# A windowed attention and feed-forward kernel: scores over 64 rows, values by three query blocks, loads by feature halves, and a planner that counts instructions

## Chip, cores and metric

The kernel runs on one core of a Trainium2 chip. The metric is the time of the program on the device in microseconds, the median of several runs; lower is better. A core has a matrix engine (TensorE, PE in the profile), a vector engine (VectorE, DVE), a scalar engine (ScalarE, ACT), GpSimd (POOL) and a sequencer that issues DMAs (SyncE, SP). Every engine works through its own instruction queue in order.

## What is computed

Attention over 8 batches, 8 heads, 576 positions and 64 features, in which a query sees the keys within 32 positions of it and 8 global positions, and the queries of the global positions see every key. Its result, 4608 tokens of 512 features, goes through a feed-forward layer of width 2048 with softplus.

```python
scores = scale * np.matmul(q, k.transpose(0, 1, 3, 2))
mask = np.abs(pos[:, None] - pos[None, :]) <= window
mask = mask | is_global[:, None] | is_global[None, :]
scores = np.where(mask, scores, -1000000000.0)
attn = np.exp(scores - np.max(scores, axis=-1, keepdims=True))
attn = attn / (np.sum(attn, axis=-1, keepdims=True) + 1e-09)
attn_out = np.matmul(attn, v)
x = attn_out.transpose(0, 2, 1, 3).reshape(B * S, H * D)
h = x @ w_in
g = np.maximum(h, 0.0) + np.log1p(np.exp(-np.abs(h)))
return g @ w_out
```

## The kernel before

**Tiles.** A batch's 576 positions are 18 blocks of 32; the 8 batches make 144 blocks. Four blocks in a row are a *pair* (its 8 heads lie as two halves, so the tile has two planes), four pairs are a *stage* of 512 tokens, and there are nine stages. The stages' values and feed-forward products are numbered m = 0 to 8.

**Loads.** For each batch, `load_qk` (line 241) brings q and k into `stage0` and `stage1`, two heads to a group of 32 partitions: four DMAs for each tensor, 2,304 contiguous pieces of 512 bytes. `load_v` (246) brings v in eight DMAs of 256-byte pieces. All are issued from SP's queue, apart from half of the first batch's q and k, which go out from ScalarE's. The output stores (813) stand in SP's queue too. GpSimd issues the weights' loads (843, 847). A batch's q and k can be loaded only after the batch before has been cast out of the same buffer.

**Preparing a batch.** q, k and v are cast to bf16 (line 414, the copy helper, on ScalarE, GpSimd or VectorE). `turn` (474, 484, 486) transposes q and k in 32 by 32 blocks on VectorE. `pick` (495) gathers the global positions' rows of q and k with 144 small products (each with a weight load); `tg` and `fill` put the picked keys into the slots between the blocks of `kx`. A query block thus finds its own block, its two neighbours and the global keys in four neighbouring slots of 32.

**Scores.** `sc` (622) computes a pair's scores: for each block, 2 halves of the features by 8 heads, products of 32 rows by 32 columns over 128 columns, two of which add up to one head's scores. The first four pairs add the mask with a third product (the identity with the mask); the others add it on VectorE (629). Then on VectorE the maximum (639), on GpSimd the difference (647), on ScalarE the exponential (660), on VectorE the sum and its reciprocal (667, 669), on GpSimd the product with the reciprocal (676, `pn`), and on VectorE a transpose (686, `pt`).

**Global queries.** `sg` (548) computes their scores against all keys, in three products (two feature halves, then the row mask), `mx` and `gexp` (556, 565) the maximum and the exponential with its sum (read from ScalarE's accumulator), `tpg` (577) the transpose, `ov` (585) the product with v, per head half and block, and `gv` (590) the division.

**Values.** `val` (770) forms a stage's attention output in four PSUM banks: for each two query blocks one product with the global values `vg` and up to four with key blocks, each for 2 halves by 4 groups, 32 rows by 64 columns, over 32 or 64 columns. `xev` copies them to bf16 (`xT`).

**Feed-forward.** Per stage 64 products of 512 columns with w_in (795, `h`), 16 softplus (801, `g`), and 64 products with w_out (806, `o`), copied out (`osb`) and stored. (The first stage does its h in two halves of 256 columns.)

**The order.** The class `_Order` is a planner that runs while the program is built. Each piece of work names its engine or engines with a cost, the pieces it needs, the PSUM banks and buffers it opens, and a rank; the planner lays pieces one after the other, the one that can start first, and emits them in that order, so each engine's queue is fixed at build time. Pairs run one ahead of the stage whose values they feed. The exponentials of a stage wait for the last softplus of the stage before (`gate`), since both use ScalarE's function table, which has to be loaded at each change. A change of the array's tile size costs `SWITCH` in the planner. The planner knows nothing of the number of instructions.

Of the kernel before, what the change touches and what calls it, by code (L numbers as in the profile page):

```python
# [18 lines left out]
class _Order:  # L19
# [15 lines left out]
    SWITCH = 95  # L35

    def add(self, cost, emit, deps=(), rank=5, opens=(), uses=(), table=None, moves=0, array=128, urgent=False):

        job = dict(cost=cost, emit=emit, deps=[d for d in deps if d is not None], rank=rank, opens=list(opens),
                   table=table, moves=moves, array=array, urgent=urgent, n=len(self.jobs), at=None, end=None)  # L40
# [37 lines left out]

    def run(self, free):
# [12 lines left out]
        dma = dict(SP=0, POOL=0)  # L92
        while ready:
# [6 lines left out]
            for j in ready:  # L100
# [11 lines left out]
                for e in j["cost"]:  # L112
                    t = max(t0, free[e])
                    rank = j["rank"]
                    if e == "PE" and array != 128:
                        rank = 0 if j["array"] == array else rank + 1
# [19 lines left out]
            if e == "PE" and j["array"] != array:  # L136
                array = j["array"]
                t += self.SWITCH
# [25 lines left out]
def kernel(  # L164
# [20 lines left out]
    R = 4  # L185
    BL = 32
# [4 lines left out]
    NE = NJ + NJ // 3 + 3  # L191
    NEP = NE + 4
# [6 lines left out]
    KG = 16  # L199
# [7 lines left out]
    PARTED = 4  # L207
    HALVED = 1
# [5 lines left out]
    def col_of(r, h):  # L214
        return r ^ h

    def e_of(m):
        return 2 + m + m // 3 if m >= 0 else 0

    def first_slot(j):  # L220
        return e_of(j - 1) if j % 3 else e_of(j) - 2

    PREV = (0, 0, 0)
    SELF = (2, 1, 1)
    NEXT = (3, 2, 3)
    GLOB = (1, 3, 2)
# [10 lines left out]
    stage = [const([P, 2 * NC, 2, D], FP32, f"stage{w}") for w in range(2)] + [const([P, 2, NJ, D], FP32, "stage2")]  # L237

    def load_qk(eng, b, w, rs):
        for r in rs:  # L240
            eng.dma_start(out=stage[w][quad(r), :, :, :].rearrange("i c e d -> i c (e d)"),  # L241
                          in_=SRC[w][b, 2 * r:2 * r + 2].rearrange("h (c i e) d -> i (h c) (e d)", i=BL, e=2))

    def load_v(eng, b, h, rs):
        for c in rs:
            eng.dma_start(out=stage[2][quad(c), h, :, :],  # L246
                          in_=SRC[2][b, 2 * col_of(c, h) + h].rearrange("(m i) d -> i m d", i=BL))
# [9 lines left out]
    qb = const([P, 2 * NC, D, 2], BF16, "qb")  # L257
    kb = const([P, 2 * NC, D, 2], BF16, "kb")
    vb = [const([P, 2, NJ, D], BF16, f"vb{i}") for i in range(2)]
    qx = [const([P, 2, 2, S], BF16, f"qx{i}") for i in range(2)]  # L260
    kx = [const([P, 2, 2, NEP * BL], BF16, f"kx{i}") for i in range(2)]
    qg = [const([P, 2, 2, BL], BF16, f"qg{i}") for i in range(2)]
    vg = [const([P, 2, D], BF16, f"vg{i}") for i in range(2)]
    pg = const([P, 2, NC, BL, 2], BF16, "pg")
    pgt = const([P, 2, NC, BL, 2], BF16, "pgt")
    mask = const([P, NJ + 2, SL, BL], BF16, "mask")
    pick = const([P, NC, 2, KG + BL], BF16, "pick")
# [21 lines left out]
    nc.gpsimd.memset(mask[:].rearrange("p j s i -> p (j s i)"), NEG)  # L289
    for i in range(2):  # L290
        for h in range(2):
            for w in range(2):
                clear(nc.gpsimd, kx[i][:, h, w, 0:BL])
                clear(nc.gpsimd, kx[i][:, h, w, (NE - 1) * BL:NE * BL])

# [20 lines left out]
    def make_pick():  # L316
# [5 lines left out]
        V.tensor_tensor(out=pick[:].rearrange("p c e g -> p (c e) g")[:, :, KG:KG + NG],  # L322
                        in0=over(posK[:].rearrange("p c e -> p (c e)"), NG), in1=under(gf[:], 2 * NC), op=OP.is_equal)

# [16 lines left out]
    def make_near():  # L341
# [4 lines left out]
        for a in range(3):  # L346
            V.tensor_scalar(out=mask[:, a:NJ:3, GLOB[a], 0:NG], in0=eqF[:, a:NJ:3, :], scalar1=-0.5, scalar2=-2 * NEG,
                            op0=OP.add, op1=OP.mult)
            V.tensor_scalar(out=mask[:, a:NJ:3, GLOB[a], KG:KG + NG], in0=near[:, a:NJ:3, :], scalar1=NEG, scalar2=None,
                            op0=OP.mult)  # L350

    BANDS = ((0, 0, 1, 0), (0, 2, 4, 1), (1, 0, 3, 0), (2, 0, 2, 0), (2, 3, 4, 2))

    def make_slots(e, x):
        a, s0, s1, x = BANDS[x]
        n = (s1 - s0) * BL
        copy(e, mask[:].rearrange("p j s i -> p j (s i)")[:, a:NJ:3, s0 * BL:s1 * BL], under(band[:, x * BL:x * BL + n], NJ // 3))

    def make_ends():
        nc.gpsimd.memset(mask[:, 0, 0, :], NEG)  # L360
        nc.gpsimd.memset(mask[:, NJ - 1, SL - 1, :], NEG)
        nc.gpsimd.tensor_copy(mask[:, NJ:NJ + 2, :, :].rearrange("p j s i -> p (j s i)"),
                              mask[:, 0:2, :, :].rearrange("p j s i -> p (j s i)"))

    def make_rows():
        V.tensor_scalar(out=oh[:], in0=pos[:, 0:NG], scalar1=pi[:, 0:1], scalar2=None, op0=OP.is_equal)
        clear(V, sel[:])
        V.tensor_copy(sel[:, KG:KG + NG], oh[:])  # L368
# [13 lines left out]
    ST, PNB, PTB = 6, 2, 8  # L382
    SLOTS = dict(xT=2, osb=2, st=ST, pn=PNB, pt=PTB, gt=2, small=2)
# [50 lines left out]
    def add_load(b, w, deps):  # L434
# [5 lines left out]
        else:  # L440
            T["load", b, w] = o.add({"DMA": (1800, 0)}, lambda e: load_qk(nc.sync, b, w, (0, 2, 1, 3)), deps, rank=0,
                                    moves=4300)

    def add_cast(b, w):
# [5 lines left out]
        for h in range(2):  # L450
            def emit(e, h=h):
                if w == 2:
                    copy(e, vb[b % 2][:, h, :, :], stage[2][:, h, :, :])
                else:
                    c = slice(h * NC, (h + 1) * NC)
# [7 lines left out]
    def add_prep(b):  # L463
        i = b % 2
        late = []
        if b >= 2:
            late = [T["sc", n] for n in pairs_of(b - 2)] + had(("sg", b - 2))
        rank = 10 * phase_of(b) + 4

        def turn(e, w):  # L470
            if w == 0:
                x = qb[:].rearrange("p c d e -> p c (d e)").bitcast(I32).rearrange("p (h c) (w i) -> p h c w i", h=2, w=2)
                y = qx[i][:].bitcast(I32).rearrange("p h w (c i) -> p h c w i", i=BL)
                V.transpose(out=y, in_=x)
                return
            x = kb[:].rearrange("p c d e -> p c (d e)").bitcast(I32).rearrange("p (h a t) (w i) -> p h a t w i", h=2, t=3, w=2)
            y = kx[i][:].bitcast(I32)
            HB = BL // 2
            A = NC // 3

            def to(e0):
                return y[:, :, :, e0 * HB:(e0 + 8 * A) * HB].rearrange("p h w (a x) -> p h a w x", a=A)
            for t, e0 in ((0, 2), (2, 7)):
                V.transpose(out=to(e0)[:, :, :, :, 0:BL], in_=x[:, :, :, t, :, :])
            for h in range(2):
                V.transpose(out=to(4)[:, h].rearrange("p a w (s i) -> p a w s i", i=HB)[:, :, :, 0:4:2, :],
                            in_=x[:, h, :, 1, :, :])

        def pck(e, w):
            ps = PS["pick", b, w] = psum(("pick", b, w), [P, 2, D], FP32)  # L490
            g0 = 0 if w else KG
            for c in range(NC):
# [455 lines left out]
```

## Time and profile before

| | us |
|---|---|
| median of three runs | 472.97 |
| lowest, highest | 469.99, 476.07 |
| the profiled execution | 470.99 |
| its span, first to last instruction | 469.3 |

The granted TensorE clock averaged 0.886 over the span. The page of the profile lists each engine's busy time, the chain of work that ended last (followed back from the last instruction, each step to what released it), the costliest groups of instructions by line, and DMA queues with packets and bytes. "issue" in the chain is time in which the engine waited for nothing that the profile shows. In rows of the chain the columns are start, length, engine and line, and how many instructions were merged; in timelines a row also has the operation, what it writes and reads, and the idle time before it.

### The profile page before, as it was taken

Reading aid. Unit: us, or ns where it says so; the run is one execution under the profiler, and the core shown is the slowest. Engines: PE = TensorE matmul, PEld = TensorE weight load, DVE = VectorE, ACT = ScalarE, POOL = GpSimd, SP = SyncE. Lnnn points to the kernel's source line nnn. Section 1 sums busy time; section 2 is a strip of 40 time slices with the busy share of each in tenths; the row PEclk is TensorE's granted clock in tenths of the full one; section 3 lists DMA queues with packets and bytes.
Section 4 is the critical chain, followed back from the end, with each engine's and each line's share of the span. In section 5 each row is a group of like instructions: output and inputs, shape, how many; then the busy total and the mean of one; then the engine's idle time right before and its main releaser. Section 6 shows DMA issues by size and latency. Waiting matters only on the chain.

```text
span 469.3 us, 19736 instructions
## 1 busy us (share of the span) xinstructions
PE 362.0 (77%) x9038; PEld 206.2 (44%) x9088; DVE 247.3 (53%) x448; ACT 220.7 (47%) x410; POOL 173.2 (37%) x136
## 2 busy tenths in 40 slices
PE   0434359992999678966897799759977977996996
PEld 0423347652555434443544454534544444443442
DVE  7647229592777672667248545745656175031101
ACT  4264135962658046803672358226704561670630
POOL 5327216471663471246205551443334334022000
PEclk9955559996899979995999799979978999998899
DMA  8999991853788138314551311140110010001001
GB/s 181 198 213 213 194 178 38 165 143 86 150 174 208 48 82 168 82 49 103 119 108 50 92 38 40 54 105 1 50 39 10 1 70 27 24 23 47 24 24 67
DMA packets 85412, 43.23 MB, mean 92 GB/s; under 512 B 39760, under 2 KB 80720, under 8 KB 85328
## 3 DMA queue, kind: packets, MB, share of 16 engines
q1 hardware_dynamic: 78736, 36.59, 35.0%
q0 software_dynamic: 4224, 4.19, 5.3%
q10 hardware_dynamic: 2368, 1.18, 1.1%
q8 instruction: 71, 1.16, 1.1%
q14 instruction: 13, 0.11, 0.1%
HBM read 36.71 MB, written 9.44 MB: 98 GB/s over the span
## 4 chain that ended last, share of the span: by engine, by line
PE 74%; issue 16%; SPq 5%; DMA 3%; POOL 1%; DVE 1%; ACT 0%; ACTq 0%; POOLq 0%
PE o L806 28%; PE h L795 27%; PE xo L770 6%; PE s L622 5%; PE pick L495 4%; DMA stage<-in_k_dram 3%; PE ov L585 3%; SPq L241 2%; SPq L246 2%; PE sg L548 1%; POOL kb L414 1%; DVE xT L414 0%; ACT kb L414 0%; ACT g L801 0%; DVE osb L414 0%
## 5 line engine op out<-in xcount | busy, mean ns | idle before, releaser
L806 PE MATMUL o<-wout,g 128*128 128x512 bf16 x544 | 133.5, 398 | 11.9 <-issue 11.4
L795 PE MATMUL h<-xT,win 128*128 128x512 bf16 (+1 forms) x622 | 135.3, 370 | 3.5 <-issue 2.2
L676 POOL TENSOR_TENSOR pn<-st,rs 128x1024 bf16<-128x1024 f32 (+1 forms) x40 | 69.4, 1743 | 131.9 <-DVE rs L669 120.0
L801 ACT ACTIVATE g<-h 128x512 bf16<-128x512 f32 (+1 forms) x160 | 85.2, 560 | 65.6 <-PE h L795 45.0
L795 PEld LDWEIGHTS <-win 128*128 128x128 bf16 x640 | 63.0, 101 | 68.0 <-issue 11.8
L806 PEld LDWEIGHTS <-g 128*128 128x128 bf16 x576 | 56.3, 101 | 80.7 <-issue 22.8
L647 POOL TENSOR_TENSOR st<-st,m 128x1024 f32<-128x1024 f32 x32 | 60.5, 1896 | 81.5 <-DVE m L639 81.5
L414 DVE COPY osb<-o 128x512 f32<-128x512 f32 x25 | 16.9, 674 | 67.2 <-PE o L806 57.1
L629 DVE TENSOR_TENSOR st<-s,mask 128x512 f32<-128x512 f32 x64 | 41.8, 675 | 11.5 <-PE s L622 11.3
L622 PE MATMUL s<-kx,qx 32*32 32x128 bf16 x2304 | 33.9, 248 | 15.6 <-issue 15.1
L667 DVE TENSOR_REDUCE sm<-st 128x8 f32<-128x1024 f32 x32 | 38.2, 1193 | 13.6 <-ACT st L660 13.6
L770 PE MATMUL xo<-pt,vb 32*64 32x64 bf16 (+1 forms) x2176 | 26.7, 210 | 23.5 <-issue 23.5
L414 ACT CAST xT<-xo 128x512 bf16<-128x512 f32 (+1 forms) x22 | 10.4, 532 | 70.4 <-PE xo L770 70.4
L414 DVE CAST xT<-xo 128x512 bf16<-128x512 f32 (+1 forms) x18 | 11.1, 656 | 54.3 <-PE xo L770 54.3
L639 DVE TENSOR_REDUCE m<-st 128x8 f32<-128x1024 f32 x32 | 38.6, 1206 | 0.2
L622 PEld LDWEIGHTS <-qx 32*32 32x32 bf16 x2304 | 26.2, 98 | 20.9 <-issue 20.6
L770 PEld LDWEIGHTS <-vb 32*64 32x64 bf16 x2176 | 24.4, 110 | 24.7 <-issue 24.5
L495 PEld LDWEIGHTS <-pick 32*32 32x32 bf16 x1152 | 20.2, 101 | 30.1 <-issue 11.8
L660 ACT ACTIVATE st<-st 128x1024 f32<-128x1024 f32 x32 | 32.1, 1054 | 0.1
L686 DVE STREAM_TRANSPOSE pt<-pn 128x512 int32<-128x512 int32 (+1 forms) x40 | 25.5, 639 | 5.0 <-POOL pn L676 5.0
L414 ACT COPY osb<-o 128x512 f32<-128x512 f32 x11 | 6.4, 582 | 45.7 <-PE o L806 27.6
L495 PE MATMUL pick<-kb,pick 32*32 32x128 bf16 x576 | 11.7, 236 | 16.8 <-DVE sel L368 12.6
(86 smaller groups left out, 341.8 us busy)
## 6 DMA issues: line engine op xcount, KB each, us to landing
stage<-in_v_dram SPq DMA_DIRECT2D x64, 144.0 KB, 3.7
out_dram<-osb SPq DMA_DIRECT2D x36, 256.0 KB, 2.0
stage<-in_k_dram SPq DMA_DIRECT2D x30, 288.0 KB, 6.1
stage<-in_q_dram SPq DMA_DIRECT2D x30, 288.0 KB, 7.1
win<-in_moe_w_in_dram POOLq DMA_DIRECT2D x4, 512.0 KB, 11.2
wout<-in_moe_w_out_dram POOLq DMA_DIRECT2D x4, 512.0 KB, 14.7
stage<-in_k_dram ACTq DMA_DIRECT2D x2, 288.0 KB, 6.3
stage<-in_q_dram ACTq DMA_DIRECT2D x2, 288.0 KB, 10.7
```

What stands on the lines that cost most here:

```text
L414: {"ACT": nc.scalar.copy, "DVE": V.tensor_copy, "POOL": nc.gpsimd.tensor_copy}[e](out, in_)
L495: nc.tensor.matmul(out=ps[quad(r), :, :], lhsT=pick[quad(r), c, x, g0:g0 + BL], rhs=(qb, kb)[w][quad(r), :, :, x].rearrange("p (h c) d -> ...
L622: nc.tensor.matmul(out=PS["s", n, h][quad(col_of(r, h)), x, :], lhsT=qx[b % 2][quad(r), h, w, j * BL:(j + 1) * BL] if w < 2 else eye[quad( ...
L629: V.tensor_tensor(out=PS["st", n][:, h, :, :], in0=PS["s", n, h][:, :, :], in1=mask[:, j0:j0 + PB, :, :].rearrange("p j s i -> p j (s i)") ...
L639: V.reduce_max(out=m[:], in_=PS["s", n, h0][:] if masked else flat(PS["st", n], h0, h1), axis=AX)
L647: nc.gpsimd.tensor_tensor(out=t, in0=t, in1=over(PS["m", n, y][:], SL * BL), op=OP.subtract)
L667: V.reduce_sum(out=sm[:], in_=flat(PS["st", n], h0, h1), axis=AX)
L676: nc.gpsimd.tensor_tensor(out=pn[:, h0:h1].rearrange("p h x u i w -> p (h x u) w i"), in0=PS["st", n][:, h0:h1].rearrange("p h x (u w i) - ...
L770: nc.tensor.matmul(out=PS["xo", v_, r][h * D:(h + 1) * D, c0 + x0 * BL:c0 + (x0 + nx) * BL], lhsT=vg[i][quad(c), h, :] if key is None else ...
L795: nc.tensor.matmul(out=h[:, :], lhsT=w_in_t[c // 4][:, kd, c % 4 * P:(c % 4 + 1) * P], rhs=PS["xT", m][:, kd, lo:hi], start=(kd == 0), sto ...
L801: nc.scalar.activation(out=PS["g", m, c][:, lo:hi], in_=PS[key][:, :], func=AF.Softplus)
L806: nc.tensor.matmul(out=PS["o", m, ns][:, :], lhsT=PS["g", m, kf][:, ns * P:(ns + 1) * P], rhs=w_out_t[kf // 4][:, kf % 4, :], start=(kf == ...
```

## The change

**Heads by feature halves.** Two groups of four heads (`HG`) replace four groups of two. `load_qk` now puts one half of a head's 64 features into one group of 32 partitions and the other half into the next, so that 64 partitions hold a head's features. A contiguous piece is 128 bytes, and there are eight DMAs to a tensor and batch in place of four, with 9,216 pieces in place of 2,304.

```diff
-            eng.dma_start(out=stage[w][quad(r), :, :, :].rearrange("i c e d -> i c (e d)"),
-                          in_=SRC[w][b, 2 * r:2 * r + 2].rearrange("h (c i e) d -> i (h c) (e d)", i=BL, e=2))
+            g, f = divmod(r, 2)
+            for e in range(2):
+                eng.dma_start(out=stage[w][quad(r), :, e, :],
+                              in_=SRC[w][b, HG * g:HG * g + HG].rearrange("a (c i e) (f d) -> e f i (a c) d", i=BL, e=2, f=2)[e, f])
```

**Scores in one product.** A head's scores for a block are one product over 64 rows where they were two over 32. The masked pairs add the mask with one more product, over 64 rows of which half are zero. The global scores go the same way.

```diff
-                for w in range(2 + masked):
-                    for h in range(2):
-                        for r in range(R):
-                            nc.tensor.matmul(out=PS["s", n, h][quad(col_of(r, h)), x, :],
-                                             lhsT=qx[b % 2][quad(r), h, w, j * BL:(j + 1) * BL] if w < 2 else eye[quad(r), :],
...
+                for w in range(1 + masked):
+                    for a in range(HG):
+                        for g in range(2):
+                            nc.tensor.matmul(out=PS["s", n, g][quad(a ^ g), x, :],
+                                             lhsT=qx[b % 2][rows(g), a, j * BL:(j + 1) * BL] if w < 1 else eye[rows(g), :],
...
```

The slots of `kx` change with it: a global slot after every two blocks instead of three, with the two halves' global keys interleaved in it; the mask gets a plane for each half. `turn` transposes k in one instruction instead of four.

**Values by three query blocks.** `pn` is written with the two halves' weights side by side as bf16 pairs, and transposed into one long tile `pt` for the whole stage, in which the blocks are laid so that the three query blocks that meet a key block stand at one constant step. One product then covers up to three query blocks (96 columns) for a key block, and one the global values of all blocks of a batch in the stage. `val` is cut into four pieces of work that the planner may set apart.

```diff
+            for k_ in range(max(j - 1, 0), min(j + z - x + 1, NJ)):
+                lo, hi = max(k_ - 1, j), min(k_ + 2, j + z - x)
+                steps.append((b, k_, x + lo - j, x + hi - j, False, k_ == min(j + z - x, NJ - 1)))
...
+                            lhs = vb[i][quad(c), key, h * D:(h + 1) * D]
+                            slot = NEXT[x % 2] if key > j else SELF[x % 2] if key == j else PREV[x % 2]
+                            rhs = run(c, h, x, slot, [[2 * (STEP - BL - BL // 2), z - x]] if z - x > 1 else [])
```

**Global values.** `ov` takes both halves at once: one product for a block and group over 129 columns (both halves' values and a column of ones that gives the sum), 72 products in place of 144, cut in two pieces of work. The sum no longer comes from ScalarE's accumulator.

```diff
-                        nc.tensor.matmul(out=ps[quad(c), h, :], lhsT=pgt[quad(c), h, m // 2, :, m % 2],
-                                         rhs=vb[i][quad(c), h, m, :], start=(m == 0), stop=(m == NJ - 1))
...
+                    nc.tensor.matmul(out=ps[quad(c), :], lhsT=pgt[quad(c), m, 0:2 * NG, :].rearrange("p g h -> p (g h)"),
+                                     rhs=vb[i][quad(c), m, 0:2 * D + 1], start=(m == 0), stop=(m == NJ - 1))
```

**`pick`** keeps its 144 products per batch but is laid as three pieces of work for each tensor.

**The planner counts instructions.** A piece of TensorE work carries the number of its instructions (`ins`). The planner supposes that instructions come in blocks of 256, each a fixed time after the one before, and sets work back that would run into the end of a block by more than `NEAR`.

```diff
+    BLOCK = 256
+    FETCH = 3600
+    NEAR = 150
+    def stall(self, t, took, ins):
+        held = 0
+        at, ready, n = self.edge, self.fetched, self.issued
+        while n + ins >= at:
+            here = t + held + took * (at - n) / max(ins, 1)
+            held += max(0, ready - here)
+            ready = max(ready, here) + self.FETCH
+            at += self.BLOCK
+        return held, at, ready
...
+                        held = self.stall(t, j["cost"][e][0], self.size(j))[0]
+                        t += held if held > self.NEAR else 0
```

More of the change, by code (lines that the diff above doesn't have):

```diff
@@ L92, in run @@
         dma = dict(SP=0, POOL=0)
+        self.edge, self.fetched, self.issued = 193, 0, 0
         while ready:
@@ L135, in run @@
                 t += 1290
[L136 removed]
+            if e == "PE":
+                t += self.SWITCH if array != j["array"] else 0
                 array = j["array"]
[L138 removed]
+                n = self.size(j)
+                held, self.edge, self.fetched = self.stall(t, step, n)
+                t += held
+                self.issued += n
             if j["moves"]:
@@ L483, in turn @@
[L483 to L492, printed above, removed]
+            y = kx[i][:, :, 2 * BL:(2 + 3 * NC) * BL].bitcast(I32).rearrange("p a (c x) -> p a c x", x=3 * HB)[:, :, :, 0:BL]
@@ L588, in gv @@
         def gv(e):
-            for h in range(2):
-                V.tensor_scalar(out=vg[i][:, h, :], in0=PS["ov", b][:, h, :], scalar1=PS["grs", b][:, h:h + 1],
-                                scalar2=None, op0=OP.mult)
+            rs = sb.tile([P, 1], FP32, tag="grs", name="grs")
+            V.reciprocal(rs[:], PS["ov", b][:, 2 * D:2 * D + 1])
+            V.tensor_scalar(out=vg[i][:], in0=PS["ov", b][:, 0:2 * D], scalar1=rs[:, 0:1], scalar2=None, op0=OP.mult)
         rank = 10 * phase_of(b) + 1
-        T["sg", b] = o.add({"PE": (800, 965)}, sg, had(("turn", b, 1), ("gev", b), "make_rows") + gate, rank=3, array=32,
-                           opens=[("sg", key) for key in keys] + [("small", ("gsm", b))])
```

374 lines of the change are left out of this document (194 added, 180 removed).

## The prediction

> **What bounds the kernel now.** I read the page first (busy shares, chain of waits), then the chain in order of time, cut at the point where the second stage of the feed-forward part begins, then the windows and the DMA view.
>
> ```profile
> span 469.3 us, 19736 instructions
> ...
> PE 362.0 (77%) x9038; PEld 206.2 (44%) x9088; DVE 247.3 (53%) x448; ACT 220.7 (47%) x410; POOL 173.2 (37%) x136
> ...
> q8 instruction: 71, 1.16, 1.1%
> ...
> PE 74%; issue 16%; SPq 5%; DMA 3%; POOL 1%; DVE 1%; ACT 0%; ACTq 0%; POOLq 0%
> ```
>
> TensorE carries the chain: 74% is matmuls, and 16% of 469.3 (75 us) is "issue", time in which TensorE waits for nothing that the profile can name. The other engines are busy 53% and less. The program lists 18,178 instructions for TensorE before and 11,826 after; the instruction queue moved 1.16 MB in 71 packets, so one packet is 256 instructions (18,178/71).
>
> ```profile
> 104.10 1.15 PE xo L770 x117
> 105.25 4.58 issue
> 109.84 1.34 PE xo L770 x106
> 111.17 2.39 issue
> 113.56 0.76 PE xo L770 x33
> ```
>
> Here the products of keys' values run with nothing between them. From one stop's end to the next it is 3.72 us (109.84 to 113.56), and in that time some 128 products with their 128 weight loads pass (a few records are missing): 256 instructions, one packet, that need 1.3 us to run. So I read "issue" as TensorE running out of instructions: a packet of 256 arrives at best every 3.7 us. A large matmul buys time for the fetch, a small one doesn't.
>
> To test this I cut the order of the old program at every 256 TensorE instructions, priced each piece by the rows below, and summed what each falls short of 3.7 us.
>
> ```profile
> 98.13 1.28 PE ov L585 x144
> ...
> 102.97 1.13 PE pick L495 x72
> ...
> 121.24 0.66 PE s L622 x64
> ...
> 159.55 2.09 PE xo L770 x225
> ...
> 191.84 0.86 PE sg L548 x48
> ...
> 357.07 1.91 PE o L806 x4
> ...
> 377.49 5.78 PE o L806 x26
> ```
>
> Per product, with its weight load: ov 8.9 ns, pick 15.7, s 10.3, xo 9.3, sg 17.9, and 222 for a full matmul of 512 columns. From 118.56 us to the end the pieces fall short by 50.8 us (26 of 52 pieces). The chain of that stretch says:
>
> ```profile
> by line: PE o L806 33.7%; PE h L795 32.0%; issue 14.2%; PE xo L770 5.8%; PE s L622 5.6%; PE pick L495 3.3%; PE ov L585 2.4%; PE sg L548 1.4%; ACT kb L414 0.4%; ACT g L801 0.2%; DVE osb L414 0.2%; ACTq L414 0.0%
> ```
>
> 14.2% of 350.7 is 49.8 us. The count fits, though it leaves the short stops at changes of stage no room of their own; so it is good to some us, not better.
>
> **Part by part: from 118.56 us on.** Small products: s 1600 to 864, xo 2136 to 1104, ov 864 to 432, sg 288 to 192, pick 720 to 840 (some move from the start into this stretch). An s product over 64 rows still has 128 columns, and eight of them (two row halves by four outputs) use the array that eight of 32 rows used, so I keep 10.3 ns; bounds are the 8.9 of the ov row and the 15.7 of the pick row, which has four places in use. The xo products are longer (96 columns at most, the shared global ones up to 512), at 9.3 as now. An ov product has 129 columns where it had 64, on the same four places: I take 15.7, the pick row's 128 columns. Sum 60.5 us before, 42.6 after; the chain shows 18.5% of 350.7, 64.9 us, so scaled by 64.9/60.5 it is 64.9 to 45.7, a gain of 19.2 (with s at 15.7 ns, 14).
>
> Stops: the same cut of the new order has 9 of 35 pieces short, by 8.0 us together, since the planner now lays picks, scores and the four parts of the values between large matmuls. Gain 49.8 - 8.0 = 41.8. Changes between large and small work go from 92 to 116; the "issue" crumb at such a change is
>
> ```profile
> 90.68 0.16 issue
> ```
>
> in the chain, so +4.
>
> What is late next is the softmax loop: scores of the next stage can only be exponentiated after the last softplus.
>
> ```profile
> 331.65 1.28 ACT L660 ACT_TABLE_LOAD   x1
> ...
> 346.27 0.70 DVE L686 STREAM_TRANSPOSE pt<-pn 128x512 int32<-128x512 int32 x1
> ...
> 350.73 0.23 PE L770 MATMUL xo<-pt,vg 32*64 32x64 bf16 x8
> ```
>
> From the table load to the third transposed block (all that the values need) are 15.3 us; xo started 3.8 us later, so the loop is covered now. After, TensorE has 64 x 0.222 + 0.6 (sg) + 1.1 (ov) + 0.3 (s) = 16.2 us in that place. A bare cover; I charge 0.5 us in each of eight stages, +4. The edits on VectorE, ScalarE and GpSimd (one transpose of k for four, no accumulator reads, mask twice as deep) lie off the chain, under the 0.2 to 0.4% that those engines have in it. Sum: 350.7 - 19.2 - 41.8 + 4 + 4 = 297.7.
>
> **Part by part: the first 118.56 us.**
>
> ```profile
> 30.09 7.08 DMA stage<-in_k_dram
> 37.32 2.92 POOL kb L414 x2
> 40.28 1.03 PE pick L495 x30
> 41.32 2.25 issue
> ...
> 46.05 4.00 issue
> ...
> 52.37 3.04 issue
> ...
> 56.97 2.72 PE h L795 x12
> ...
> 64.59 2.10 PE pick L495 x55
> ...
> 68.52 1.99 issue
> ...
> 73.27 0.69 issue
> ...
> 116.09 1.21 issue
> ...
> 118.56 2.67 PE h L795 x8
> ```
>
> Loads set the pace to 37 us, stops from there. And the loads get dearer: q and k come in pieces of 128 bytes, 9,216 of them per tensor and batch for 2,304 of 512. The trace has no such piece; it has 256 bytes (the DMA view of v alone, 80 to 86.2 us, first row) and 512 (of q and k, 179 to 192 us, second); columns are packets, MB and share of 16 engines.
>
> ```profile
> q1 hardware_dynamic: 4736, 1.18, 100.5%
> ```
>
> ```profile
> q1 hardware_dynamic: 4736, 2.36, 92.9%
> ```
>
> That is 6.2 x 16/4736 = 21.0 ns per piece of 256 bytes and 0.929 x 13 x 16/4736 = 40.8 ns for 512: time goes by bytes. For 128 the ends are 10.2 (bytes alone) and 21.0 (a piece costs no less than the 256-byte one); I take 14, nearer the end that both rows point to. A load then takes 8.1 us for 5.9, +2.2 (0 to +6.2). The Trainium skill weighs against this edit: DMA: Bandwidth & Descriptors, Specifications, asks for 512 bytes or more for full rate; here 256 bytes reached it. The same page (How a descriptor splits into AXI transactions; Why small descriptors are slow) has a piece that starts in the middle of 256 bytes fetch from their start, as every second piece here does; estimated by its beats, 17 ns per piece, and the total below 406; no row shows such a piece.
>
> k of batch 1 lands after three such loads: 37.2 + 6.6 = 43.8, cast to 46.7, first h near 48 for 56.97, since the stops between go (in the new order 1,266 TensorE instructions precede that h, 1,890 before). q of batch 1 shares the engines with v and w_out: two load times later, 59, cast 62, where TensorE stood at 64.59. From there to the next stage's h it was 54.0 us: less 10.9 of stops (1.99, 0.69, 4.58, 2.39, 1.21), of which 1 stays, less small products 13.0 to 6.3, less 3.8 for 24 h of 256 columns and 5 o that now run ahead: 33.6, and 2 for the softmax loop. So that h starts at 98.
>
> SP issues eight DMAs per load where it issued four:
>
> ```profile
> L241 SPq DMA_DIRECT2D stage<-in_k_dram x30: 311/496/6941, 1.2 to 229.1; - x30
> ```
>
> At 0.5 us each that is 4 us; behind them queue the output stores, with two buffers, and TensorE meets them only through a full bank. No charge.
>
> 98 + 297.7 = 396; the execution had 470.99 for a span of 469.3, so 397.4, and the median of the runs lies 2 above that execution: **398**.
>
> **Rivals.** (1) *The softmax loop decides.* The weights of a pair are normalized and transposed into strided places; if that adds 3 us to the loop beyond what I charged, xo waits 3 us in seven stages: 398 + 21 = 419. For: cover of only 0.9 us. Against: VectorE's busy time per stage leaves room (us of the stretch, then busy time of TensorE, its weight loads, VectorE, ScalarE and GpSimd, granted clock, DMA):
>
> ```profile
> 314.30:359.00 44.70, 38.92 (x876) 20.49 (x880) 24.41 (x43) 20.36 (x34) 14.26 (x9) 0.88 0.08 27
> ```
>
> (2) *Loads decide, and it ends slower.* 147,456 pieces of q and k, and beside them:
>
> ```profile
> q1 hardware_dynamic: 78736, 36.59, 35.0%
> q0 software_dynamic: 4224, 4.19, 5.3%
> ```
>
> Queue 1 had 164 us; q and k are 88 of it (34,560 x 40.8/16), v 48 (36,864 x 21.0/16), stores the rest, and queue 0, the weights, 25. At 40.8 ns per piece, the 512-byte price, the loads take 376 + 48 + 25 = 449 us, and behind the last one come a stage of 36 and the final one:
>
> ```profile
> 437.40:469.30 31.90, 27.89 (x127) 12.41 (x127) 3.46 (x5) 10.57 (x17) 0.00 (x0) 0.98 0.11 42
> ```
>
> 449 + 36 + 32 + 4 (span to median) = 521, slower. It decides from 37 ns per piece up. For: nothing shows 128 bytes. Against: halving 512 halved the price.
>
> (3) *The fetch takes 6 us, as between the stops that end at 43.57 and 50.04*, because denser loads hold the DMA engines longer. The pieces then fall short by 39.1 instead of 8.0: 429.
>
> (4) *Stops aren't fetches*, and the change doesn't remove them. Then only the products' 19.2 and the start's 9.8 (25.4 to 15.6) go, with 4 for the changes: 473 - 29 + 4 = 448. The Trainium skill would have it so: Runtime: NRT & Kernel Launch, Instruction fetch mechanics, calls crossing a block of 256 instructions mostly hidden. The five rows at 104 us, with 1.3 us of work and 3.7 from block to block, disagree.
>
> (5) *The clock comes back.* It was 0.88 of full in the window above; a full matmul costs 478 ns at 357.07 and 222 at 377.49. If without long stops it stays up, eight stages save 1 us each (four products at 222 for 478) and the twelve h at 56.97 (227 ns each for half of 222) 1.4: 389.
>
> **Numbers.** Forecast 0.61, (1) 0.15, (3) 0.07, (5) 0.08, (4) 0.03, (2) 0.04, and 0.02 for losses that eat all gains (several of these together). The range of the forecast by its own bounds (s at 8.9 to 15.7 ns; pieces at 10.2 to 21 ns, which five loads of the start pay one after the other) is 386 to 423; with (5), (1) and the edge of (3), 380 to 428 holds 8 in 10. Faster by over 2%, which is about what a measurement of this kernel tells from none (under 463.5), 0.94; within 2%, 0.02; slower, 0.04.
>
> **What would show it.** Instruction packets near 46; "issue" in the chain at 20 to 35 us in all; s at 10 ns per product; a q or k load at 8 us; the h of the second stage at 98 us; 36 to 37 us from stage to stage. Wrong if VectorE's transposes or DMA take over the chain, or if the stops stay though the packets fell.

## The result and the profile after

The changed kernel takes 392.34 us (median; 392.31 to 394.3) where the kernel before, run beside it, takes 474.52 (469.99 to 476.24). The ratio is 0.829, with a 95% interval of 0.822 to 0.836. The forecast was 398. The profiled execution took 392.31 us for a span of 390.6.

The page of the changed kernel: span, busy time by engine, the queue that carries q, k and v, the instruction queue (packets, MB, share), and the chain by engine.

```profile
span 390.6 us, 13430 instructions
...
PE 323.6 (83%) x5858; PEld 172.7 (44%) x5912; DVE 235.1 (60%) x406; ACT 221.9 (57%) x386; POOL 170.7 (44%) x129
...
q1 hardware_dynamic: 183376, 36.59, 49.6%
...
q8 instruction: 46, 0.75, 0.8%
...
PE 57%; DVE 20%; SPq 11%; DMA 4%; POOL 4%; issue 2%; ACT 2%; POOLq 0%; ACTq 0%; DVEq 0%
```

Instruction packets went from 71 to 46 and "issue" in the chain from 16% of 469.3 us (75 us) to 2% of 390.6 (8 us). But TensorE no longer carries the chain alone: VectorE has 20% of it (1% before), SP's DMA issues 11% (5% before). So the stops went, and something else was late next.

Where that is, the stages tell. From the first softplus of a stage to that of the next (first to eighth stage) it was 60.7, 51.6, 50.0, 46.5, 48.3, 44.5, 41.4 and 37.0 us; now it is 38.3, 51.2, 43.4, 39.3, 34.8, 33.1, 34.8 and 29.0. The windows view of the changed kernel, for the second to fourth stage and for the fifth to eighth (us; busy time of TensorE, its weight loads, VectorE, ScalarE, GpSimd; clock; DMA):

```profile
95.47:190.16 94.69, 80.25 (x1698) 41.48 (x1706) 69.09 (x106) 53.83 (x75) 45.68 (x27) 0.93 0.87 155
229.46:361.13 131.67, 127.93 (x1859) 63.05 (x1880) 75.90 (x122) 81.82 (x124) 54.37 (x30) 1.00 0.18 52
```

Late stages are TensorE and nothing else: 128 of 132 us, at full clock. In the early ones the DMA engines are busy 0.87 of the time and TensorE misses 14 of 95 us. Three places show what is waited for. First the start, in the chain (start, length, engine and line):

```profile
33.29 5.94 SPq L269
...
39.28 3.87 SPq L269
...
43.20 3.79 DMA stage<-in_k_dram
...
47.21 1.46 POOL kb L451
48.67 0.98 POOL pn L699
...
53.72 1.10 PE xo L799 x68
...
56.21 1.66 PE h L827 x12
```

A load of q or k is eight DMAs, and SP stands 4 to 7 us on each of four of these eight; the trace doesn't say for what. k of batch 1 lands at 47. GpSimd's own timeline (idle time before, and its releaser, in brackets) shows who pays:

```profile
47.19 1.48 POOL L451 CAST kb<-stage 128x1152 bf16<-128x1152 f32 x1 [17.94 <-DMA stage<-in_k_dram]
48.60 3.04 POOL L699 TENSOR_TENSOR pn<-st,rs 128x512 bf16<-128x512 f32 x3
```

The first stage needs nothing of batch 1. Its `pn` merely stands behind that batch's cast in GpSimd's queue, and the values (`xo`) and the first h wait for `pn`. What `pn` itself needs was there 10 us before; VectorE's timeline:

```profile
38.13 0.17 DVE L693 RECIPROCAL rs<-sm 128x4 f32<-128x4 f32 x1
```

The same thing happens to ScalarE and TensorE later. ScalarE's timeline:

```profile
135.91 1.48 ACT L451 CAST qb<-stage 128x1152 bf16<-128x1152 f32 x1 [8.96 <-DMA stage<-in_k_dram]
...
137.63 1.56 ACT L451 CAST xT<-xo 128x512 bf16<-128x512 f32 x3
```

and TensorE's:

```profile
151.07 0.42 PE L646 MATMUL s<-kx,qx 64*32 64x128 bf16 x32
155.59 0.80 PE L525 MATMUL pick<-qb,pick 32*32 32x128 bf16 x24 [4.10 <-POOL qb L451]
156.72 2.85 PE L827 MATMUL h<-xT,win 128*128 128x512 bf16 x7 [0.33 <-issue]
```

Here `xT`, ready to be copied, stands behind a cast that waits 9 us for a load of a batch to come, and TensorE 5.2 us for that `xT`; and h products whose `xT` is there stand behind a pick of such a batch.

### The profile page after: what moved, and what is told of

It reads as the page before. It is cut to its first block, busy times and chain, and to the rows that moved or that the text cites. A ratio compares the mean times of both kernels' runs of the same rounds, so it can differ in the third digit from the quotient of the medians.

```text
span 390.6 us, 13430 instructions
## 1 busy us (share of the span) xinstructions
PE 323.6 (83%) x5858; PEld 172.7 (44%) x5912; DVE 235.1 (60%) x406; ACT 221.9 (57%) x386; POOL 170.7 (44%) x129
## 3 DMA queue, kind: packets, MB, share of 16 engines
q1 hardware_dynamic: 183376, 36.59, 49.6%
## 4 chain that ended last, share of the span: by engine, by line
PE 57%; DVE 20%; SPq 11%; DMA 4%; POOL 4%; issue 2%; ACT 2%; POOLq 0%; ACTq 0%; DVEq 0%
PE h L827 27%; PE o L838 20%; SPq L269 10%; DVE st L653 4%; DVE sm L691 3%; PE pick L525 3%; DVE m L663 3%; DVE pt L708 3%; PE xo L799 2%; DMA stage<-in_k_dram 2%; POOL pn L699 2%; PE s L646 2%; PE ov L607 2%; DMA stage<-in_q_dram 1%; DVE gm L587 1%
## 5 line engine op out<-in xcount | busy, mean ns | idle before, releaser
L838 PE MATMUL o<-wout,g 128*128 128x512 bf16 x543 | 127.8, 381 | 4.3 <-issue 3.7
L833 ACT ACTIVATE g<-h 128x512 bf16<-128x512 f32 (+1 forms) x160 | 84.9, 557 | 46.7 <-PE h L827 33.4
L838 PEld LDWEIGHTS <-g 128*128 128x128 bf16 x576 | 53.8, 98 | 64.4 <-issue 2.2
L451 DVE COPY osb<-o 128x512 f32<-128x512 f32 x21 | 14.3, 683 | 59.1 <-PE o L838 46.4
L691 DVE TENSOR_REDUCE sm<-st 128x8 f32<-128x1024 f32 x32 | 38.0, 1189 | 16.5 <-ACT st L684 16.5
L708 DVE STREAM_TRANSPOSE pt<-pn 128x512 int32<-128x512 int32 x36 | 25.0, 694 | 13.4 <-POOL pn L699 13.3
L680 ACT ACTIVATE st<-s,m 128x128 f32<-128x128 f32 x32 | 11.3, 374 | 22.2 <-DVE m L665 19.0
L451 ACT COPY osb<-o 128x512 f32<-128x512 f32 x15 | 8.8, 585 | 26.0 <-PE o L838 14.8
L646 PE MATMUL s<-kx,qx 64*32 64x128 bf16 x1152 | 18.4, 234 | 4.2 <-DVE st L653 2.6
L587 DVE TENSOR_REDUCE gm<-sg 128x1 f32<-128x320 f32 (+1 forms) x32 | 13.1, 449 | 12.3 <-PE sg L579 12.3
L451 POOL CAST kb<-stage 128x1152 bf16<-128x1152 f32 x7 | 10.4, 1489 | 21.3 <-DMA stage<-in_k_dram 17.9
L531 DVE STREAM_TRANSPOSE gt<-pick 128x128 f32<-128x128 f32 x16 | 4.9, 308 | 23.6 <-PE pick L525 23.6
```

Of the source, the lines that this page charges most:

```text
L451: {"ACT": nc.scalar.copy, "DVE": V.tensor_copy, "POOL": nc.gpsimd.tensor_copy}[e](out, in_)
L691: V.reduce_sum(out=sm[:], in_=flat(PS["st", n], h0, h1), axis=AX)
L708: V.transpose(out=bass.AP(base.tensor, base.offset, ap=[list(base.ap[0]), [2 * STEP, PB // 2], [STEP + BL // 2, 2], [1, SL * BL]]), in_=PS ...
L833: nc.scalar.activation(out=PS["g", m, c][:, lo:hi], in_=PS[key][:, :], func=AF.Softplus)
L838: nc.tensor.matmul(out=PS["o", m, ns][:, :], lhsT=PS["g", m, kf][:, ns * P:(ns + 1) * P], rhs=w_out_t[kf // 4][:, kf % 4, :], start=(kf == ...
```

## The experiments

Two theories had to be told apart, and a third came up. A: TensorE stopped because a block of 256 instructions is there at best 3.7 us after the one before; the cut of the order at every 256, as in the prediction, tells how long it stops. B: the stops have another cause, or only the order matters. C: what is late next (loads, VectorE) sets the time, so that TensorE's counts no longer matter. From experiment 5 on the letters are those of each expectation. Ratios are to the kernel before, run beside each.

**1. The planner doesn't count.**

```diff
-        held = 0
+        return 0, self.edge, 0
```

> The changed kernel, with the planner's count of instructions taken out again: the same 11,826 TensorE instructions, the same products and loads, only their order differs. Theory A (TensorE runs out of instructions: a block of 256 is there at best 3.7 us after the one before): cut at every 256, this order falls short by 11.4 us up to the second stage's h and by 11.6 us after it, for 11.4 and 8.0 in the changed kernel, so 392 + 4 = 396 us (393 to 401). Rival B (the order is what removed the stops, as the change's last part says): most of the 42 us of stops come back, 415 us or more. Rival C (loads and VectorE set the pace now, TensorE's order no longer matters): 392, within 1%.

Measured: 381.09 us, ratio 0.802 (0.796 to 0.808): *faster* than the changed kernel, which none of the three expected; the intervals are apart. "issue" in the chain stays at 2%. So the counting is not what removed the stops. In TensorE's timeline the pick that held it up at 155.59 above now stands behind the stage's last h and costs 0.82 us:

```profile
162.68 1.21 PE L525 MATMUL pick<-qb,pick 32*32 32x128 bf16 x72 [0.82 <-POOL qb L451]
```

The second and third stage together take 85.9 us for 94.7. That is where most of the 11 us lie. In the start this order has the first stage's `pn` ahead of the cast in GpSimd's queue:

```profile
36.14 3.04 POOL L699 TENSOR_TENSOR pn<-st,rs 128x512 bf16<-128x512 f32 x3 [4.70 <-DVE rs L693]
47.50 2.88 POOL L451 CAST kb<-stage 128x1152 bf16<-128x1152 f32 x2 [8.32 <-DMA stage<-in_k_dram]
```

The load is no earlier (47.3 for 47.0), but the first h comes 5.2 us behind it in place of 9.2. In the other runs on the changed kernel that are reported below it comes 8.0 to 9.1 us behind it where those `pn` stand behind the cast (five runs), 4.9 to 7.5 where they stand ahead of it (three). That the 11 us are the count's doing, and not one lucky order, isn't shown: see 9.

**2. The old kernel with the counting planner.** The planner's lines as in the change; values, picks and global values cut into pieces with their counts (`VCUT` is 2):

```diff
...
+        for u0 in range(0, units, VCUT):
+            last = o.add({"PE": (VCUT * 165, VCUT * 165 + 170)}, lambda e, u0=u0: val(e, u0, u0 + VCUT), ready if last is None else [last],
+                         rank=1, array=64, urgent=last is None, ins=80 * VCUT, opens=opened if last is None else [],
...
```

The first try:

> The kernel before with the counting planner alone: same products, loads and tiles as before, 18,178 TensorE instructions; values cut in four pieces of work, picks in three, global values in four, each with its count. Theory A: with so many instructions no order helps. Cut at every 256 this order falls short by 41.6 us up to the second stage's h and 44.7 after it, for 29.6 and 50.8 in the kernel before: 471 + 6 = 477 us (465 to 482). Rival B (the order does it): the stops after the start go, 42 us, so about 430.

Measured: 535.27 us, ratio 1.126 (1.118 to 1.133). The values' pieces had been given 30,720 instructions in place of 160, so the time says nothing of the count. With the true numbers:

> The kernel before with the counting planner alone, now told the true counts: 18,178 TensorE instructions, products, loads and tiles as before; values cut in four pieces of work of 160 instructions, picks in three of 48, global values in four of 72. (In the earlier run under this name but the 2 at its end the planner was told 30,720 instructions and 127 us for each stage's values, so that its order was no test of the count.) Cut at every 256 this order falls short by 29.0 us up to the second stage's h and 41.0 after it; the kernel before by 29.6 and 50.8. Theory A (too many small instructions for any order to hide): 10 us less than the kernel before at the most, 460 to 474. Rival B (the order is what removes stops): 42 us less, 430. Rival C (the count's setting back costs more than the stops it avoids, as at 11,826 instructions, where leaving it out gained 11 us): 474 to 485.

Measured: 479.64 us, ratio 1.015 (1.008 to 1.022), as C said. From the first softplus of the second stage to the end "issue" falls from 49 to 31 us, so the count does remove stops. They come back in another place. The chain of this kernel in its first stage (s is line 659, pick 523, xo 809):

```profile
111.42 2.89 issue
...
116.08 4.15 issue
...
123.09 2.07 issue
...
128.59 2.05 issue
...
132.44 1.65 issue
```

The planner had spread the large products thin and early; by 110 us none was left, and the scores and values that the next stage needs ran bare, a stop to each 256. That stage took 80.7 us for 60.7.

**3. Score products twice.**

```diff
-                for w in range(1 + masked):
+                for w in [-1] + list(range(1 + masked)):
...
```

> The changed kernel with each product of q and k issued twice into the same place (the first is overwritten by the second, the output is the same); the planner is told so. 2,304 instructions more, 14,130 in all, 55 packets for 46. Theory A: pieces of 256 fall short by 20.2 us up to the second stage's h and 7.0 after it, together 27.2 for 19.4, so 7.8 more; the products take 1,152 x 10.3 ns = 11.9 us: 392 + 20 = 412 us. Rival B (instructions cost only the time of their products): 392 + 12 = 404, and with s at its 7.4 ns 401. Rival C (TensorE is not what sets the pace): 392 to 398.

Measured: 404.42 us, ratio 0.851 (0.845 to 0.857), 12 us more than the change and nearer to rival B: in sum the 1,152 further products cost the time they take. The stops that theory A added lay in the start (20.2 for 11.4), where loads are late anyway; behind it the cut says 7.0 us for 8.0, and "issue" there is 2.6 us. That fits an instruction that large products hide costing only its product, but doesn't show it: the second stage starts 17.1 us later than in the change and the rest is 5.6 us shorter, so work moved in the order is mixed into the 12 us.

**4. Values by two query blocks,** with the count, and without it:

```diff
-            z = min(X1, x + NJ - j)
+            z = min(X1, x + NJ - j, x + 2)
```

> The changed kernel with the values met by two query blocks again: a run of blocks is cut after every two, so a stage has the 2,752 products of the kernel before where the change has 1,432; all else as changed. 14,466 instructions, 57 packets for 46. Theory A: pieces of 256 fall short by 20.5 us up to the second stage's h and by 17.7 after it, 38.2 for 19.4, so 18.8 more; the products take 1,320 x 9.3 ns = 12.3 us: 392 + 31 = 423 us (412 to 428). Rival B (products' time alone): 404. Rival C (TensorE does not set the pace): 392 to 398.

> Both undone: the values met by two query blocks and the planner not counting; 14,466 TensorE instructions. Beside the run with two blocks and a counting planner (419 us) it tells what the count is worth where there are more instructions, and beside the run without the count (381 us) what the three-block products are worth by themselves. Cut at every 256 this order falls short by 18.2 us up to the second stage's h and 30.7 after it (with the count 20.5 and 17.7; without the count but with three blocks 11.4 and 11.6). Theory A (short pieces stop TensorE wherever they come, and the count's loss at 11,826 instructions comes from elsewhere, the late global scores): after the start 19 us of stops and 12 of products more than 381: 412 us, and 'issue' at 20 us or more in the chain. Rival B (the count costs 11 us however many instructions there are, and stops hardly matter): 381 + 12 = 393 to 400, 'issue' as in the run without the count.

Measured: 419.29 us (0.882; 0.876 to 0.888) and 426.9 us (0.900; 0.896 to 0.904). With the count the three-block products are worth 27 us, without it 46, and at 14,466 instructions the count gains 8 us where at 11,826 it lost 11. Both are far from rival B's 404 and 400, though theory A's 412 for the second was 15 short, for which no cause is shown. The chain of the two kernels, by line, from the second stage's first softplus to the end (with the count first):

```profile
by line: PE h L827 34.6%; PE o L838 33.2%; PE xo L799 5.5%; SPq L269 4.4%; issue 3.4%; PE pick L525 3.3%; PE ov L607 2.3%; PE s L646 2.2%; DVE st L653 1.5%; DVE m L663 1.1%; PE sg L579 1.0%; DMA stage<-in_q_dram 0.9%; DVE xT L451 0.9%; DVE 
```

```profile
by line: PE h L827 36.0%; PE o L838 29.0%; issue 9.5%; PE xo L799 6.2%; PE pick L525 3.8%; PE s L646 3.0%; DVE sm L691 2.8%; PE ov L607 1.8%; DVE gm L587 1.5%; DVE qg L451 1.0%; PE sg L579 1.0%; DVE pgt L599 0.6%; DVE pt L708 0.5%; DVE rs L
```

3.4% of 310.1 us is 10.5, 9.5% of 324.0 is 30.8. Read the same way in every order, the cut against the chain:

| order | instructions | short by the cut, us | "issue" in the chain, us |
|---|---|---|---|
| before | 18,178 | 50.8 | 49 |
| before, counting (2, first run) | 18,178 | 44.7 | 36 |
| before, counting (2, second run) | 18,178 | 41.0 | 31 |
| two blocks, no count | 14,466 | 30.7 | 31 |
| two blocks | 14,466 | 17.7 | 10.5 |
| no count | 11,826 | 11.6 | 3.7 |
| changed | 11,826 | 8.0 | 6.8 |
| scores twice | 14,130 | 7.0 | 2.6 |

Both columns are from the second stage on. The cut errs by up to 10 us and mostly says too much, perhaps since a piece that is short can be hidden under another wait, but it follows the stops from 3 to 50 us over eight orders. The second column has an error of its own: experiment 6 runs the order of the kernel before with other loads, and "issue" there is 39 us for 49. In the start, where loads are late, the cut fails: 11.4 us for the changed kernel, under 2 in the chain.

Where the stops stand settles what they are. TensorE's weight loads are all in the traces, and each has one product, so two instructions to a load give the place in the program. In the kernel before, all 30 pieces of "issue" over 0.7 us in the chain end at the same place in the count by 256, 182 to 190 instructions into it; over the eight orders it is 94 of 99. So theory A stands; the Trainium skill's sentence that crossing a block of 256 is mostly hidden (Runtime: NRT & Kernel Launch, Instruction fetch mechanics) holds here only where large products fill the block.

**5. The load part undone, all else in the same order.**

```diff
-            for e in range(2):
-                eng.dma_start(out=stage[w][quad(r), :, e, :],
...
+            eng.dma_start(out=stage[w][quad(r), :, :, :].rearrange("i (x y) e d -> i x (y e d)", y=2),
...
```

> The changed kernel in the same order, with q and k loaded in the four DMAs and the 512-byte pieces of the kernel before; the features then lie in other places than the products suppose, so the output is another, but every instruction beside the loads is as changed. A load should take 5.9 us alone for 7.5 to 8. Theory A (a load's 128-byte pieces lose against the 1 KB pieces of the weights, and the loads are the longest thing up to the second stage and again in the stages after it): k of batch 1 lands near 37 for 47 and the whole gains 10 to 25 us: 367 to 382. Rival B (only the start gains, what comes after is set by VectorE): 383 to 388. Rival C (loads are hidden): 392.

Measured: 379.41 us, ratio 0.803 (0.799 to 0.808), as theory A had it: the load part, eight DMAs of small pieces, costs 13 us (what of it is the pieces and what the number of DMAs, no run tells). The first softplus comes at 47.16 for 57.16 us, the second stage's at 87.83 for 95.47, the fourth's at 176.46 for 190.16; from the fifth stage on the stages are alike to 0.1 us. SP's time on k of batch 1, changed kernel and this one:

```profile
17.68 27.19 SPq L269 DMA_DIRECT2D stage<-in_k_dram  x8
```

```profile
16.46 13.80 SPq L267 DMA_DIRECT2D stage<-in_k_dram  x4
```

**6. Eight DMAs in the old kernel.**

```diff
+            for e in range(2):
+                eng.dma_start(out=stage[w][quad(r), :, e, :].rearrange("i c (f d) -> i c f d", f=2),
...
```

> The kernel before with q and k loaded in eight DMAs of 128-byte pieces into the same places, all else as before. It prices the load part of the change by itself. Theory A (loads count while they are the longest thing, and the kernel before has stops of TensorE beside them): +1.8 us for each of the five loads that the start pays, and some 10 us for k of batch 1 beside the weights, of which the stops hide a part: 475 + 5 to 19, 480 to 494. Rival B (hidden): 475. Rival C (every load counts): 475 + 16 x 1.8 = 504.

Measured: 469.02 us, ratio 0.996 (0.992 to 0.999). It missed its aim. Queue 1 (packets, MB, share) has

```profile
q1 hardware_dynamic: 114256, 36.59, 37.7%
```

35,520 packets more than the kernel before, where the change has 104,640 more (183,376 less 78,736): two runs of 128 bytes that lie behind each other at both ends went as one, and the pieces were of 256 bytes. So this prices eight DMAs and halved pieces in the old kernel, at nothing; pieces of 128 bytes weren't tried there.

**7. w_out's load behind the cast of batch 1's k.**

```diff
-            load_batch(1)
+            make_batch(1)
...
-                                      [T["w_in", 3], T.get(("w_out", a - 1))], rank=4, moves=3100)
+                                      [T["w_in", 3], T.get(("w_out", a - 1)), *T["cast", 1, 1]], rank=4, moves=3100)
```

> The changed kernel with the loads of w_out (2.1 MB, four DMAs from GpSimd) put behind the cast of batch 1's k instead of behind w_in; nothing else is asked for. Theory A (k of batch 1 is starved by the weights beside it): k lands near 37 for 47, the first h comes near 46 for 56, and the whole gains 5 to 10 us: 382 to 387. Rival B (behind the first h the next loads, then VectorE from 69 to 94 us, set the second stage anyway): 390 to 394.

Measured: 385.11 us, ratio 0.816 (0.811 to 0.820), within theory A's 382 to 387.

```profile
17.63 16.77 SPq L269 DMA_DIRECT2D stage<-in_k_dram  x8
```

SP is through with k in 16.8 us for 27.2 and the first softplus comes 8.8 us earlier, so the weights' load did starve it. But the second stage starts 5.4 us *later* (100.84 for 95.47): the head start is spent before it, as rival B said. The 7 us come from the second and third stage, 83.5 us for 94.7; why they are shorter isn't shown.

**8. Eight pairs masked by TensorE.**

```diff
-    PARTED = 4
+    PARTED = 8
```

> The changed kernel with the mask of eight pairs instead of four added by TensorE (128 products more, 256 instructions); for those four pairs VectorE doesn't add the mask nor sum, GpSimd doesn't subtract, and ScalarE takes 16 exponentials of 128 columns in place of one of 1,024. Theory A (from 69 to 94 us VectorE and GpSimd carry the chain: 17 and 8 us): VectorE loses about 2 us in each of four pairs, GpSimd 1.9: 8 us off, +1 on TensorE: 385. Rival B (ScalarE's exponentials, some 2 us more in each pair and between the softplus, take their place): 392 to 400.

Measured: 393.33 us, ratio 0.832 (0.827 to 0.837), the time of rival B. The second stage starts 10.7 us later, the next two are 12.7 us shorter together. Rival B's reason isn't seen: ScalarE has 1 us of the chain in the longer stretch up to the second stage. So this relief for VectorE, with the order that came with it, buys nothing in sum; what the relief is worth by itself stays open.

**9. Both gains together (the edits of 1 and 7), and with a truer price for loads in the planner.**

```diff
-                                    moves=7000)
+                                    moves=9500)
```

> The changed kernel with the planner not counting and the loads of w_out put behind the cast of batch 1's k. Each alone gave 381 and 385 us for 392. Theory A (they act at different places, the first on the stages behind the start, the second on the start): 392 - 11 - 7 = 374 us. Rival B (both shift the same wait for the next batch's loads, so only the larger counts): 381.

> As the run before it, and the planner supposes 9,500 ns for a load of q or k, as the chip needs in the first stages, where it supposed 7,000; the work itself is the same. Theory A (in the stages behind the start picks and casts stand in their queues ahead of their data, and hold up what is behind them): the waits of GpSimd and TensorE for loads at 50 to 160 us shrink, 3 to 6 us less than that run: 368 to 371. Rival B (the loads themselves are late, whatever stands behind the wait): the same time within 2 us.

Measured: 387.08 us (0.816; 0.813 to 0.819) and 383.58 us (0.811; 0.807 to 0.815). Neither theory: the sum is worse than the better part. With w_out late, leaving the count out changes nothing (387 for 385); without, it gained 11 us. The truer price takes 3.5 us off, with intervals that overlap. So edits that only move work in the order shift the time by some 10 us, and the count's worth at 11,826 instructions can't be told from that. The fastest kernel that computes all of it (experiment 5's has the features in the wrong places) is that of experiment 1, 3% below the change.

## Why the prediction was right

**Stops.** -41.8 us was expected from the second stage on; "issue" there went from 49 to 6.8. Right in size and, by the table and the place of the stops, in cause. Rivals (3) and (4) fall. Packets: 46, as forecast. The sign of 20 to 35 us of "issue" in all was too high: 8. And that few stops are left doesn't need the planner's count: without it the chain has 3.7 us (experiment 1). Fewer instructions, and work cut into pieces that can be set apart, are what both orders share; experiment 4 shows the instructions' part.

**Small products.** The chain of the seventh stage:

```profile
311.55 0.61 PE sg L579 x32
...
318.10 0.35 PE s L646 x32
...
319.20 1.16 PE ov L607 x72
...
324.56 1.29 PE xo L799 x115
```

Per product with its weight load s takes 10.9 ns (10.3 was taken), ov 16.1 (15.7), sg 19 (17.9), xo 11.2 (9.3). The -19.2 us were too much by some 3: 1,104 xo at 1.9 ns more are 2.1 us, s, sg and ov together 0.9.

**Pieces of 128 bytes.** Nearly all of queue 1 between 57.5 and 74 us is such pieces (135 bytes in the mean):

```profile
q1 hardware_dynamic: 16116, 2.18, 85.2%
```

0.852 x 16.5 us x 16/16,116 is 14.0 ns each, the value taken; the 17 ns estimated from the Trainium skill (DMA: Bandwidth & Descriptors, How a descriptor splits into AXI transactions; Why small descriptors are slow) were too dear. Rival (2) falls with it.

**What failed: the start, and what the loads hold up.** k of batch 1 was to land at 43.8 and came at 47; its cast was to end at 46.7 and ended at 48.7. But the first h was to come near 48, right behind that cast, and came at 56.2, as late as before (56.97). The step took the cast for the last thing that h waits for. Behind it, as the chain above has it, stand `pn`, four microseconds on VectorE (transposes with maxima of later pairs between them), `xo` and a pick: 7.5 us. With `pn` ahead of the cast it is 5.2 us from the load's landing to h (experiment 1) where the prediction had 4.2.

The second stage's h still came at 93.2, before the forecast 98, and that is luck. The prediction's path to it ran over the cast of batch 1's q, forecast to end at 62; it ended at 61.6, so the late first h cost nothing there. Of the 35.6 us from that cast to h, the prediction gave TensorE all but 2; of the 31.7 measured, the chain has 23 on VectorE and GpSimd:

```profile
72.56 1.12 DVE m L663
...
79.81 1.14 DVE sm L691
...
81.32 1.91 POOL pn L699
...
87.85 1.78 POOL pn L699
```

For the loads the prediction charged 2.2 us each to the five of the start, and nothing for SP's issues or for later loads. By experiment 5 the load part costs 10.0 us at the first softplus (three loads, 6.6 charged), 7.6 at the second stage's (11 charged) and 13.7 at the fourth's.

**What was mis-sized: the softmax loop and the stages.** +4 us were charged for all stages, 36 to 37 us forecast for each. VectorE has 20% of the chain, most of it before 230 us, so rival (1) came true in the second to fourth stage (44.7 us in the mean) together with the waits for loads. The fifth to eighth took 32.9 us in the mean. Rival (5) came true there: the granted clock was 1.00, where the prediction's window had 0.88; but at the rival's price that is 1 us a stage, and the rest of the shortfall isn't broken down. The two errors cancel: seven stages were to take about 267 us (297.7 less the 29.5 of the last one and 1.2 from h to softplus) and took 265.7. The time was right partly by that luck. What in the early stages is due to VectorE and what to loads isn't settled: experiment 8 relieved VectorE and gained nothing in sum, experiment 5 relieved the loads and gained 13 us with VectorE's work as it was.

**Slips in the sums.** Two load times of 8.1 us behind 43.8 end at 60, not 59; 397.4 and 2 are 399, not 398; five loads at 17 ns a piece give 407, not below 406; 267 us for seven stages are 38 each, not 36 to 37; and by rival (2)'s own terms loads decide from (398 - 145)/9.216 = 27 ns a piece, not 37. Put right, the first two make the forecast 400; the others leave it as it is.

## What to carry to other kernels

Where a profile shows "issue" between runs of tiny matmuls, count instructions before columns: cutting the order at each block and summing what every piece falls short of the block's time foretold the stops within 10 us or so here, and fewer, longer products removed them where reordering alone gave nothing. When a bound of that size goes, look at which in-order queue holds a step for data that is still being loaded, with work behind it that could run: here work that was ready stood 10 us behind a cast for a batch to come. And price an edit of the loads in the kernel as it will be: eight DMAs of halved pieces cost nothing in the old kernel, eight of quartered ones 13 us in the changed one.

## What the runs showed that wasn't expected

**Small pieces lose beside large ones.** The DMA view of the changed kernel from 18 to 44 us, when the weights (queue 0, pieces of 1 KB) load beside k of batch 1, and that of the kernel before from 18 to 37 us:

```profile
q0 software_dynamic: 4224, 4.19, 96.4%
q1 hardware_dynamic: 7943, 1.13, 41.3%
```

```profile
q1 hardware_dynamic: 5929, 2.29, 70.7%
q0 software_dynamic: 1643, 1.62, 50.3%
```

With 512-byte pieces (and v's of 256 among them) queue 1 got 2.29 MB in 19 us, and in the kernel of experiment 5 1.49 MB in 16 us (18 to 34 us); with pieces a quarter as long it got 1.13 MB in 26 us, though alone they run at 128/14.0 = 9 bytes a ns against 12.5. How the engines share their time between the two queues was not tested by itself.

**A count that removes stops can lose time.** At 18,178 instructions it took 18 us of stops out of the stages behind the first, and the first grew by 20 us.
